# Second layer of three batch pairs as seven block products instead of eight, with weight blocks kept in DRAM

## The chip, the core and the metric

One core of a Trainium2 chip runs the whole program. The metric is the device time of one execution in microseconds (us), the median of several. The profile is of one execution; its times count from the start of its span.

## The reference

Eight batches of 448 tokens go through attention with 12 heads of 64, and then through a layer that is applied to 128 chosen tokens of each batch:

```python
attn = softmax(scale * rmsnorm(q, g_q) @ rmsnorm(k, g_k).T) @ v     # (8, 12, 448, 64), all fp32
x = attn.transpose(0, 2, 1, 3).reshape(8, 448, 768)
scores = x @ w_gate
for b in range(8):
    top_idx = the 128 tokens of batch b with the highest score
    xe = x[b, top_idx]                         # 128 x 768
    h = maximum(xe @ w1, 0)                    # w1 is 768 x 1024
    ye = h @ w2                                # w2 is 1024 x 768
    out[b, top_idx] = x[b, top_idx] + sigmoid(scores[b, top_idx]) * ye
```

The product h @ w2 is the "second layer" of the title.

## The kernel before

**Attention.** The function `fast` does the work. A unit is one 64-key block of one group of four heads; there are 24 groups (three for each batch) of seven units, 168 units in all. For a unit, `scores` (L294) writes two PSUM tiles with 64-row matmuls, ACT takes the exponential (L303), `values` (L318) multiplies by v, and DVE adds the probabilities up (L334) for the denominators. When a group has ended, `values_out` copies its two halves from PSUM (tile `xT`), `sum_keys` (L362) sums the denominators on PE, `invert_sums` (L386, L388) inverts them, `to_tokens` (L407) transposes each half c back to token order, and DVE scales it (L409). `gate` (L433) makes the score for the choice; after the last group of a batch `score_rows` (L462, L468), `count` (L478) and `annotate` rank the tokens, `select` (L505) scatters the chosen rows to DRAM on the POOL queue, `load_selected` (L523) reads them back, and `store_x` (L421) stores the batch.

**The layers.** Batches are taken in five groups: (0), (1, 2), (3, 4), (5, 6), (7). `mixture` is a generator; each `yield` ends one *piece*. A pair has two pieces of transposes (L553), eight of the first layer (L582, moving 256 columns, both tokens' batches at once) and eight of the second layer (L601): for each batch and each half of 384 output columns, eight fp32 matmuls over the 1024 inner rows, four to a piece, into one PSUM bank. DVE then adds gate times result to the tokens (L610), and POOL writes rows out (L620). An fp32 matmul of full width is two records in the profile.

**The order of work** is written out by hand. Round q takes units 4q to 4q+3: all their scores and values, then two halves. Each half may take one piece of the layers (`piece`) and one or two waiting tasks (`opening`): a group that ends in round q has `sum_keys` due at place 1 of round q, `to_tokens` of its first half at the start of round q+1 and `last_tokens` (its second half) at place 1 of round q+1. Work in `todo` is run at its slot; slots 4q to 4q+3 belong to round q, two to each half. DMAs of the SP queue are issued in that order too. `single` says in which rounds the second half takes no piece: always while the first group is under way (rounds below BEGIN = 21), and for a pair where the count of its pieces stands at 3 or 4. Rounds start in the profile at 106.1 us (q = 12), 157.0 (17), 197.0 (21), 276.1 (28), 314.0 (31), 393.1 (38). Pair (1, 2) runs in rounds 21 to 30, pair (3, 4) in 31 to 40; pair (5, 6) and batch 7 come after the last unit, from 440 us on.

**PSUM.** Eight banks of one tile each: four for `sc` (pool `ps_sc`, scores and some others), two for `av`, one `aux` (denominators, transposes of `to_tokens`) and one `moe` (the layers). After the last unit `bank()` takes the layers' banks from `sc`.

```python
def to_tokens(n, c):
    ...
    if c == 1 and not before_layers(now[0]) and not spare[0]:
        ps = ps_sc.tile(shape, F32, tag="sc", name="x_ps")
    else:
        ps = aux(shape, "x_ps")
```

Of the kernel before, what the change touches and what calls it, by code (L numbers as in the profile page):

```python
# [68 lines left out]
def fast(  # L69
# [100 lines left out]

    wg = const.tile([CP, DM], F32, name="wg")
    w1 = const.tile([128, NDC, F], F32, name="w1")
    w2 = const.tile([128, NFC, DM], F32, name="w2")
    earlier = const.tile([CP, NJ, NJ, CP], mybir.dt.bfloat16, name="earlier")
    token_i = const.tile([CP, NJ], I32, name="token_i")
    token_f = const.tile([CP, NJ], F32, name="token_f")
# [16 lines left out]
        nc.gpsimd.tensor_copy(out=token_f, in_=token_i)  # L193

    def load_w(part):
        for w, src in ((w1, moe_w1), (w2, moe_w2)):
            n = w.shape[1]
            if part < n:
                nc.sync.dma_start(
                    out=w[:, part], in_=src.rearrange("(c p) f -> p c f", p=128)[:, part]  # L200
                )
            part -= n
            if part < 0:
                return

    def squares(n, i):
        t = get("tok", n, i)
# [127 lines left out]

    def values_out(n):
        for c in (1, 0):
            t = norm_pool.tile([128, NJ, CP], F32, name="xT", bufs=4)  # L340
            nc.scalar.copy(out=t.rearrange("d j p -> d (j p)"), in_=avs[n][c][:, 0:S])
            xTs[n, c] = t
        avs.pop(n)
# [52 lines left out]
    def to_tokens(n, c):  # L396
        b = n // NG
        if b not in xs:
            xs[b] = x_pool.tile([CP, NJ, DX], F32, name="x")
        t = xTs.pop((n, c))  # L400
        shape = [128, NJ, 128]
        if c == 1 and not before_layers(now[0]) and not spare[0]:
            ps = ps_sc.tile(shape, F32, tag="sc", name="x_ps")
        else:
            ps = aux(shape, "x_ps")
        for j in range(NJ):
            nc.tensor.transpose(out=ps[:CP, j, :], in_=t[:, j, :], identity=ident)  # L407
        col = (n % NG * 2 + c) * 128
        nc.vector.tensor_tensor(  # L409
            out=xs[b][:, :, col : col + 128].rearrange("p j (h d) -> p j h d", d=D),  # L410
            in0=ps[:CP].rearrange("p j (h d) -> p j h d", d=D),
            in1=rdens[n][:, :, :, c, None].to_broadcast([CP, NJ, 2, D]),
            op=OP.mult,
        )
# [10 lines left out]
    def gate(n):  # L425

        b, g = divmod(n, NG)
        if g == 0:
            gates[b] = moe_pool.tile([CP, NJ, NG], F32, name="gate_parts", bufs=2)
        cols = slice(GH * D * g, GH * D * (g + 1))  # L430
        for j in range(NJ):
            prod = moe_pool.tile([CP, GH * D], F32, name="prod")
            nc.vector.scalar_tensor_tensor(  # L433
                out=prod,
                in0=xs[b][:, j, cols],
                scalar=1.0,
                in1=wg[:, cols],
                op0=OP.mult,
                op1=OP.mult,
                accum_out=gates[b][:, j, g : g + 1],  # L440
            )
# [88 lines left out]
    def mixture(g):  # L530

        n, bs = CAP, groups[g]
        G = len(bs)
        wide = 128 * G
        xe = [xes.pop(b) for b in bs]
        parts_out = 1 if bs[-1] < B - 1 else 3
        xeT = moe_pool.tile([128, NDC, 2, 128], F32, name="xeT")
        hT = moe_pool.tile([128, NFC, 2, 128], F32, name="hT")

        def bank():  # L540

            if PER * now[0] >= units:
                return ps_sc.tile([128, 512], F32, tag="sc", name="sc")
            return ps_moe.tile([128, 512], F32, tag="moe", name="moe_ps")

        half = NDC // 2
        rows = []
        for i, x in enumerate(xe):
            for a in range(2):
                ps = ps_sc.tile([128, 512], F32, tag="sc", name="xeT_ps") if a else bank()  # L550
                for d in range(half):
                    dc = half * a + d
                    nc.tensor.transpose(  # L553
                        out=ps[:, 128 * d : 128 * d + n],
                        in_=x[:n, 128 * dc : 128 * (dc + 1)],
                        identity=ident[:n, :n],
                    )
                nc.scalar.copy(  # L558
                    out=xeT[:, half * a : half * (a + 1), i, :n],
                    in_=ps[:, : half * 128].rearrange("p (i t) -> p i t", t=128)[:, :, :n],  # L560
                )
                if a == 1:
                    row = moe_pool.tile([128, parts_out], I32, name="row", bufs=4)
                    for part in range(parts_out):
                        nc.vector.tensor_scalar(
                            out=row[:n, part : part + 1],
                            in0=x[:n, DM + 1 : DM + 2],
                            scalar1=float(parts_out),
                            scalar2=float(part),
                            op0=OP.mult,  # L570
                            op1=OP.add,
                        )
                    rows.append(row)
                if a == 1 or G == 1:
                    yield

        chunks = 4 // G
        for f0 in range(0, NFC, chunks):
            ps = bank().rearrange("p (i g t) -> p i g t", g=G, t=128)
            for i in range(chunks):  # L580
                for dc in range(NDC):
                    nc.tensor.matmul(  # L582
                        out=ps[:, i, :, :n],
                        lhsT=w1[:, dc, 128 * (f0 + i) : 128 * (f0 + i + 1)],
                        rhs=xeT[:, dc, 0:G, :n],
                        start=(dc == 0),
                        stop=(dc == NDC - 1),
                    )
                if i == chunks // 2 - 1:
                    yield  # L590
            nc.scalar.activation(
                out=hT[:, f0 : f0 + chunks, 0:G, :n], in_=ps[:, :, :, :n], func=AF.Relu
            )
            yield
        width = DM // max(2, parts_out)
        for i, x in enumerate(xe):
            for c0 in range(0, DM, width):
                cols = slice(c0, c0 + width)
                ps = bank()
                for fc in range(NFC):  # L600
                    nc.tensor.matmul(  # L601
                        out=ps[:n, :width],
                        lhsT=hT[:, fc, i, :n],
                        rhs=w2[:, fc, cols],
                        start=(fc == 0),
                        stop=(fc == NFC - 1),
                    )
                    if fc == NFC // 2 - 1:
                        yield
                nc.vector.scalar_tensor_tensor(  # L610
                    out=x[:n, cols],
                    in0=ps[:n, :width],
                    scalar=x[:n, DM : DM + 1],
                    in1=x[:n, cols],
                    op0=OP.mult,
                    op1=OP.add,
                )
                if parts_out > 1 or c0 + width == DM:
                    part = slice(c0 if parts_out > 1 else 0, c0 + width)
                    nc.gpsimd.indirect_dma_start(  # L620
                        out=out.flatten_outer_dims().rearrange("r (k c) -> (r k) c", k=parts_out),
                        out_offset=bass.IndirectOffsetOnAxis(
                            ap=rows[i][:n, part.start * parts_out // DM :][:, :1], axis=0
                        ),
                        in_=x[:n, part],
                        in_offset=None,
                    )
                yield

    HALVES = 2  # L630
    PER = 2 * HALVES
# [4 lines left out]
    def at(slot, fn, *args):  # L636
        todo.setdefault(slot, []).append(lambda: fn(*args))
# [31 lines left out]
    for n in range(1, n_groups):  # L669
# [4 lines left out]
        if n > 1:  # L674
# [3 lines left out]
            first = max(s0 - (20 if n > 5 else 17), 0)  # L678
            prepare(n, first)
            at(max(s0 - 6, first + 11), scale_q, n)  # L680
    for part in range(NDC + NFC):
        at(16 + 3 * part, load_w, part)
    at(7, lambda: nc.sync.dma_start(out=wg, in_=_bcast_row(moe_w_gate, CP)))
    at(11, constants)

# [17 lines left out]
    def before_layers(q):  # L703
        return done == 0 and ready.get(0, q + 1) > q

    def soon():

        q, place = now
        return PER * q + 2 * place if PER * q < units else -9
# [69 lines left out]
    def single(q):  # L779

        if q in begin:
            return pieces[0] > 0
        return PER * q < units and pieces[1] > 10 and pieces[0] in (3, 4)

    def piece(q):

# [6 lines left out]
        if ready.get(done, q + 1) > q:  # L793
            return False
        moe = mixture(done)
        pieces[:] = 1, 2 + 8 * len(groups[done])
        done += 1
        next(moe)
        return True
# [567 lines left out]
```

## Time and profile before

| what | value |
|---|---|
| runs | 513.98, 515.16, 520.19 us; median 515.16 us |
| the profiled execution | 514.41 us, of which the span is 512.6 us |
| granted TensorE clock | 1.00 of full speed |
| busy time of PE, DVE, ACT, POOL | 499.2, 333.2, 274.2, 182.7 us |
| moved by DMA | 93.21 MB |

A timeline line reads: start, length, engine, line of the kernel, operation, output from inputs, partitions of the array, shape, and the number of instructions merged; in brackets the idle time before and what ended it. Lengths of matmul groups include the drain of the last one, so distances between starts are the better measure of what PE spends. PEld is the weight load of PE; DVE, ACT, POOL and SP are VectorE, ScalarE, GpSimd and SyncE.

### The profile page before, as it was taken

To read this page: it belongs to the slowest core of one execution; us is meant where nothing else is said; L and a number is where in the kernel's file an instruction comes from. 1 tells how busy PE (TensorE), PEld (TensorE's weight loads), DVE (VectorE), ACT (ScalarE), POOL (GpSimd) and SP (SyncE) were. 2 spreads that over 40 slices of the span, in tenths; PEclk is the share of its full clock that TensorE was granted. 3 is DMA by queue.
4 is the path that set the end of the run, shared out by engine and by line. 5 is a ranking of instruction groups with operands and counts; after the bars stand their busy time and mean duration, and the time that the engine had idled before them with its cause. 6 is when DMAs were issued, how large, how long until landed. Compare 5 with 4: busy or idle time off the path is not lost. (4 is left out here: it accounts for less than half of the span.)

```text
span 512.6 us, 11058 instructions
## 1 busy us (share of the span) xinstructions
PE 499.2 (97%) x4453; PEld 287.9 (56%) x4453; DVE 333.2 (65%) x638; ACT 274.2 (53%) x507; POOL 182.7 (36%) x104
## 2 busy tenths in 40 slices
PE   5999999989999999999999999999999999999996
PEld 4544455445555445556654454656564464786595
DVE  4566899699875998697746775798564675530101
ACT  4877886775766566575455544674643434310000
POOL 5694538445424283434422435137220131020102
PEclk9999999999999999999999999999999999999999
DMA  8977889999864578468258373587221042031001
GB/s 307 375 245 254 276 284 355 320 314 319 266 214 138 191 248 276 146 216 243 68 151 264 76 259 107 177 255 191 87 85 60 9 155 71 6 125 41 31 33 36
DMA packets 43405, 93.21 MB, mean 182 GB/s; under 512 B 11059, under 2 KB 23348, under 8 KB 43346
## 3 DMA queue, kind: packets, MB, share of 16 engines
q1 hardware_dynamic: 39938, 86.11, 52.5%
q0 software_dynamic: 3264, 6.31, 3.5%
q8 instruction: 37, 0.61, 0.5%
q14 instruction: 22, 0.18, 0.1%
q10 hardware_dynamic: 144, 0.00, 0.0%
HBM read 74.93 MB, written 25.35 MB: 196 GB/s over the span
## 5 line engine op out<-in xcount | busy, mean ns | idle before, releaser
L303 ACT ACTIVATE p<-sc,rinv 128x448 f32<-128x448 f32 x336 | 186.2, 642 | 98.4 <-PE sc L294 72.6
L222 POOL TENSOR_TENSOR rinv<-ss,neg_half 128x14 f32<-128x14 f32 (+1 forms) x49 | 131.9, 2699 | 185.8 <-DVE ss L221 154.9
L294 PE MATMUL sc<-qT,kT 64*64 64x448 f32 x1344 | 155.0, 545 | 1.7 <-DVE x L409 0.8
L318 PE MATMUL av<-p,v 64*64 64x448 f32 x1344 | 148.7, 537 | 0.0
L334 DVE TENSOR_TENSOR sum<-sum,p 128x896 f32<-128x896 f32 x107 | 116.5, 1089 | 8.8 <-ACT p L303 2.9
L318 PEld LDWEIGHTS av<-p,v 64*64 64x64 f32 x1344 | 59.9, 133 | 67.5 <-issue 58.4
L294 PEld LDWEIGHTS sc<-qT,kT 64*64 64x64 f32 x1344 | 54.3, 132 | 70.0 <-issue 43.5
L221 DVE TENSOR_REDUCE ss<-sq 128x14 f32<-128x910 f32 (+1 forms) x49 | 52.1, 1074 | 18.9 <-ACT sq L212 18.9
L582 PE MATMUL moe_ps<-xeT,w 128*128 128x256 f32 (+1 forms) x288 | 56.1, 347 | 0.0
L601 PE MATMUL moe_ps<-w,hT 128*128 128x384 f32 x160 | 55.7, 491 | 0.0
L505 POOL DMA_INDIRECT selected<-x,rank x32 | 34.4, 1076 | 55.4 <-DVE x L497 47.3
L409 DVE TENSOR_TENSOR x<-x_ps,rden 112x512 f32<-112x512 f32 x48 | 32.6, 689 | 30.5 <-PE x_ps L407 29.9
L582 PEld LDWEIGHTS moe_ps<-xeT,w 128*128 128x128 f32 x288 | 46.2, 191 | 7.3 <-issue 3.2
L212 ACT ACTIVATE sq<-tok 128x896 f32<-128x896 f32 (+1 forms) x49 | 46.0, 952 | 5.2 <-DMA tok<-in_tok_dram 2.9
L433 DVE SCALAR_TENSOR_TENSOR prod<-x,wg 112x256 f32<-112x256 f32 x96 | 40.6, 423 | 3.0
L620 POOL DMA_INDIRECT out_dram<-xe,row x10 | 11.6, 1156 | 81.9 <-DVE xe L610 63.1
L601 PEld LDWEIGHTS moe_ps<-w,hT 128*128 128x128 f32 x160 | 28.8, 190 | 18.7 <-issue 2.8
L610 DVE SCALAR_TENSOR_TENSOR xe<-sc,xe 128x384 f32<-128x384 f32 (+1 forms) x7 | 3.9, 560 | 48.1 <-PE sc L601 48.1
L582 PE MATMUL sc<-xeT,w 128*128 128x256 f32 (+1 forms) x192 | 32.2, 328 | 0.3 <-ACT xeT L558 0.3
L601 PE MATMUL sc<-w,hT 128*128 128x384 f32 (+1 forms) x112 | 31.3, 440 | 0.0
L582 PEld LDWEIGHTS sc<-xeT,w 128*128 128x128 f32 x192 | 28.8, 191 | 2.9 <-ACT xeT L558 0.5
L407 PE MATMUL x_ps<-ident,xT 128*112 128x128 f32 x192 | 28.8, 276 | 0.0
(67 smaller groups left out, 293.5 us busy)
## 6 DMA issues: line engine op xcount, KB each, us to landing
tok<-in_tok_dram SPq DMA_DIRECT2D x48, 448.0 KB, 6.7
qT<-in_qT_dram SPq DMA_DIRECT2D x24, 448.0 KB, 4.6
kT<-in_kT_dram SPq DMA_DIRECT2D x24, 448.0 KB, 7.5
v<-in_vp_dram SPq DMA_DIRECT2D x24, 448.0 KB, 8.6
out_dram<-x SPq DMA_DIRECT2D x8, 1344.0 KB, 7.3
bc<-rows SPq DMA_DIRECT2D x44, 224.0 KB, 5.8
xe<-selected SPq DMA_DIRECT2D x8, 385.0 KB, 3.7
w<-in_moe_w_dram SPq DMA_DIRECT2D x6, 512.0 KB, 7.0
```

The source lines that it names most:

```text
L212: nc.scalar.activation(out=sq[:, h, :, 0:D], in_=t[:, h], func=AF.Square, scale=scale)
L221: nc.vector.tensor_reduce(out=ss[:, h], in_=sq[:, h], axis=AX.X, op=OP.add)
L222: nc.gpsimd.tensor_tensor(out=rinv[:, h].rearrange(flat), in0=ss[:, h].rearrange(flat), in1=neg_half.to_broadcast([128, (h.stop - h.start) ...
L294: nc.tensor.matmul(out=scs[hh][D * c : D * (c + 1), 0:S], lhsT=get("kT", n)[r, c, D * i : D * (i + 1)], rhs=get("qT", n)[r, c, :], start=True,
L303: nc.scalar.activation(out=p[:, hh], in_=scs[hh][:, 0:S], func=AF.Exp, scale=rinvs[n, 1][:, hh, i : i + 1],)
L318: nc.tensor.matmul(out=avs[n][c][D * hh : D * (hh + 1), 0:S], lhsT=get("v", n)[r, hh, i, :], rhs=probs[u][r, hh], start=(i == 0), stop=(i ...
L334: nc.vector.tensor_tensor(out=sums[n], in0=probs.pop(u - 1) if begins else sums[n], in1=probs.pop(u), op=OP.add)
L409: nc.vector.tensor_tensor(out=xs[b][:, :, col : col + 128].rearrange("p j (h d) -> p j h d", d=D), in0=ps[:CP].rearrange("p j (h d) -> p j ...
L433: nc.vector.scalar_tensor_tensor(out=prod, in0=xs[b][:, j, cols], scalar=1.0, in1=wg[:, cols], op0=OP.mult, op1=OP.mult, accum_out=gates[b ...
L505: w = nc.gpsimd.indirect_dma_start(out=t[:, :], out_offset=bass.IndirectOffsetOnAxis(ap=rank[:, j : j + 1], axis=0), in_=x[:, j, :], in_of ...
L582: nc.tensor.matmul(out=ps[:, i, :, :n], lhsT=w1[:, dc, 128 * (f0 + i) : 128 * (f0 + i + 1)], rhs=xeT[:, dc, 0:G, :n], start=(dc == 0), sto ...
L601: nc.tensor.matmul(out=ps[:n, :width], lhsT=hT[:, fc, i, :n], rhs=w2[:, fc, cols], start=(fc == 0), stop=(fc == NFC - 1),)
```

## The change

With A the two batches' hidden rows (two halves of the inner dimension each) and B the four blocks of w2 (inner half by column half), the second layer of a pair is a 2 by 2 block product. The change does it with seven block products of four matmuls each (Strassen's scheme in Winograd's form). Four of the weight factors are mixed blocks, T1 = B12 - B11, T3 = B22 - B12, T2 = B22 - T1 and B21 - T2. DVE makes them once (`mix`), in halves, in rounds 20 to 23; they are stored in DRAM in halves (`store_mixed`) and read back into two buffers named `ring` when the pairs need them (`load_mixed`, by way of `reload`). Three w2 blocks stay in SBUF (B11, B21, B22); B12 is read into the ring at the start and again for batch 7. The factors on the side of the tokens, s1 to s4, are made by DVE for each pair, three of them in the room of `xeT`, s4 over a11.

The products in the rounds of attention are, one to a piece: a12 B21 (own bank), a11 B11 (bank `main`, `moe`), then s2 T2 added into `main`, s1 T1 (own bank), s4 B22 (own bank), s3 T3 added into `main`, a22 (B21 - T2) added into `main`. In the text they are P2, P1, P6, P5, P3, P7 and P4 in that order; after the last unit P1 comes before P2. The banks of P2, P5 and P3 come from `sc`. Each product is followed by one eviction into the tokens (`gated`), P5 by two. A pair has 17 pieces instead of 18.

Further parts: the round without a second piece moves from counts 3 and 4 to 13 and 14; in rounds that `single` names, the second half of `to_tokens` takes the `aux` bank; `xT` has three buffers instead of four; `prod` shares the buffer of `cmp`; batch 7's output goes in column parts of 384, 256 and 128 instead of three of 256; a pair's first batch is written after P3 and its second after P4.

```diff
-    w2 = const.tile([128, NFC, DM], F32, name="w2")
+    HF, HD = NFC // 2, DM // 2
+    w2 = {b: const.tile([128, HF, HD], F32, name=f"w2_{b[0]}{b[1]}") for b in ((0, 0), (1, 0), (1, 1))}
+    mixed = [dram_pool.tile([128, HF, HD], F32, name=f"mixed{i}", bufs=1) for i in range(4)]
...
+    def in_ring(what):
+        ring[what] = moe_pool.tile([128, HF, HD], F32, name="ring", bufs=2)
+        return ring[what]
...
+    def load_mixed(i, part):
+        dst = ring[i] if part else in_ring(i)
+        nc.sync.dma_start(out=dst[:, chunk(part)], in_=mixed[i][:, chunk(part)])
+
+    def store_mixed(i, part):
+        nc.sync.dma_start(out=mixed[i][:, chunk(part)], in_=ring[i][:, chunk(part)])
+
+    def mix(i, part):
...
+        nc.vector.tensor_tensor(out=ring[i][:, f], in0=a[:, f], in1=b[:, f], op=OP.subtract)
...
-            t = norm_pool.tile([128, NJ, CP], F32, name="xT", bufs=4)
+            t = norm_pool.tile([128, NJ, CP], F32, name="xT", bufs=3)
...
-        if c == 1 and not before_layers(now[0]) and not spare[0]:
+        if c == 1 and not (before_layers(now[0]) or spare[0] or now[1] == 1 and single(now[0])):
...
+        parts_out = ((0, HD), (DM - 2 * HD // 3, DM), (HD, DM - 2 * HD // 3)) if last else ((0, DM),)
...
+        spare_room = xeT.rearrange("p c g t -> p (c g t)").rearrange("p (s f t) -> s p f t", s=3, t=128)
+        s1, s2, s3, s4 = spare_room[0], spare_room[1], spare_room[2], a11
+        for o, p, q, op in ((s1, a21, a22, OP.add), (s2, s1, a11, OP.subtract), (s3, a11, a21, OP.subtract)):
+            nc.vector.tensor_tensor(out=o[:, :, :n], in0=p[:, :, :n], in1=q[:, :, :n], op=op)
+
+        def product(ps, h, w, first=True):
+            for f in range(HF):
+                nc.tensor.matmul(
+                    out=ps[:n, :HD],
+                    lhsT=h[:, f, :n],
+                    rhs=w[:, f],
+                    start=first and f == 0,
+                    stop=(f == HF - 1),
+                    skip_group_check=True,
+                )
+
+        def side():
+            return ps_sc.tile([128, 512], F32, tag="sc", name="side_ps")
+
+        def reload(i):
+            s = soon()
+            for part in range(2):
+                at(s + 4 + 2 * part if s >= 0 else s, load_mixed, i, part)
+
+        main = ps_moe.tile([128, 512], F32, tag="moe", name="moe_ps")
+        for first in (0, 1) if PER * now[0] < units else (1, 0):
...
+            yield
+        product(main, s2, ring[2], first=False)
+        gated(0, high, main)
+        reload(3)
+        yield
+        ps = side()
+        product(ps, s1, ring[1])
+        gated(1, high, ps)
+        gated(0, high, ps)
+        reload(0)
+        yield
+        ps = side()
+        product(ps, s4, w2[1, 1])
+        gated(0, high, ps)
+        write(0, 0)
+        yield
+        product(main, s3, ring[3], first=False)
+        gated(1, high, main)
+        if g < len(groups) - 2:
+            reload(2)
+        else:
+            for part in range(2):
+                at(soon(), load_block, (0, 1), part)
+        yield
+        product(main, a22, ring[0], first=False)
+        gated(1, low, main)
+        write(1, 0)
+        if g < len(groups) - 2:
+            reload(1)
+        yield
...
+    mixing = PER * (BEGIN - 1) + 2
+    for k, i in enumerate((3, 1, 2, 0)):
+        for part in range(2):
+            at(mixing + 3 * k + part, mix, i, part)
+            at(mixing + 3 * k + part + 2, store_mixed, i, part)
+    for part in range(2):
+        at(mixing + 16 + 2 * part, load_mixed, 1, part)
...
-        return PER * q < units and pieces[1] > 10 and pieces[0] in (3, 4)
+        return PER * q < units and pieces[1] > 10 and pieces[0] in (13, 14)
...
-        pieces[:] = 1, 2 + 8 * len(groups[done])
+        pieces[:] = 1, 10 if len(groups[done]) == 1 else 17
```

## The prediction

> **What bounds the kernel.** I read the page first: its span, its busy times and the row of each engine in 40 slices.
>
> ```profile
> span 512.6 us, 11058 instructions
> PE 499.2 (97%) x4453; PEld 287.9 (56%) x4453; DVE 333.2 (65%) x638; ACT 274.2 (53%) x507; POOL 182.7 (36%) x104
> PE   5999999989999999999999999999999999999996
> DVE  4566899699875998697746775798564675530101
> PEclk9999999999999999999999999999999999999999
> ```
>
> PE is full in nearly every slice at full clock. Busy time counts drains, so I checked with distances between starts in the timeline: in a round of attention 64 records (16 scores, 16 values, twice) take 6.2 us, and rounds from 13 on are these plus their pieces, with some tenths over. So PE sets the pace, and work taken from PE shortens the time unless its place is filled by a wait. DVE is at 90% in places, so waits on DVE are what I look for.
>
> **Gross gain.** The timeline of the stretch after the last unit shows one pair's second layer with nothing between:
>
> ```profile
> 464.71 20.80 PE L601 MATMUL sc<-w,hT 128*128 128x384 f32 x64
> 485.36 0.49 PE L553 MATMUL sc<-ident,xe 128*128 128x128 f32 x3
> ```
>
> 64 records take 485.36 - 464.71 = 20.65 us, 0.3227 us each. Eight block products of four matmuls (8 records) become seven: 8 x 0.3227 = 2.58 us per pair, 7.74 us for three pairs. That is the ceiling of the main effect. The schedule does not undo it: round 30 has one piece where it had two, and the next pair still starts in round 31, since its `ready` is set by `ranks_of` in round 28 either way.
>
> **What takes some of it back.** The seven pieces stand closer together than the eight did, in one bank and in rounds without a second piece.
>
> 1. *Main bank, pair (5, 6).* P4 adds into `main` directly after P7, and must wait until DVE has read P7's result. During attention six us of scores stand between; after the last unit nothing does. The row for this eviction:
>
> ```profile
> 485.56 0.62 DVE L610 SCALAR_TENSOR_TENSOR xe<-sc,xe 128x384 f32<-128x384 f32 x1 [4.54 <-PE sc L601]
> ```
>
> It starts 0.20 us after the next matmul would start and lasts 0.62; with 0.1 to release PE, 0.92 us are lost.
>
> 2. *Aux bank, round 17.* `to_tokens` c = 1 now takes `aux` there, and `sum_keys` wants `aux` next (first PE, then DVE):
>
> ```profile
> 166.38 0.60 PE L407 MATMUL x_ps<-ident,xT 128*112 128x128 f32 x4
> 166.91 0.59 PE L362 MATMUL den_ps<-sum,pick_pair 128*32 128x112 f32 x16
> ```
>
> ```profile
> 167.01 0.69 DVE L409 TENSOR_TENSOR x<-x_ps,rden 112x512 f32<-112x512 f32 x1 [2.02 <-PE x_ps L407]
> ```
>
> The bank is free at 167.70, so L362 starts at about 167.75 instead of 166.91: 0.84 us.
>
> 3. *The same in round 38,* which is now one without a second piece (count 14):
>
> ```profile
> 402.29 0.60 PE L407 MATMUL x_ps<-ident,xT 128*112 128x128 f32 x4
> 402.73 2.75 PE L601 MATMUL moe_ps<-w,hT 128*128 128x384 f32 x8
> 405.40 0.59 PE L362 MATMUL den_ps<-sum,pick_pair 128*32 128x112 f32 x16
> ```
>
> Today 2.67 us of matmuls cover L409. In the new order P5 ends at 402.29, DVE first makes P5's two evictions (402.45 to 403.6), then L409 to 404.3; L362 follows at 404.35 instead of 402.73: 1.62 us. Of the six rounds in which `last_tokens` and `sum_keys` meet (3, 10, 17, 24, 31, 38), only 17 and 38 are `single`.
>
> 4. *Bank of P5, round 28.* The counts stand in DVE's queue ahead of P5's evictions:
>
> ```profile
> 282.26 0.59 PE L462 MATMUL row_ps<-ident,gate 112*112 112x112 f32 x4
> 285.38 0.59 PE L362 MATMUL den_ps<-sum,pick_pair 128*32 128x112 f32 x16
> 285.90 2.85 PE L601 MATMUL moe_ps<-w,hT 128*128 128x384 f32 x8
> ```
>
> ```profile
> 283.45 0.69 DVE L478 SCALAR_TENSOR_TENSOR cmp<-score_rows,gate,earlier 112x448 f32<-112x448 f32 x1 [2.82 <-ACT score_rows L468]
> 287.19 1.10 DVE L221 TENSOR_REDUCE ss<-sq 128x14 f32<-128x910 f32 x1
> ```
>
> The piece at 285.90 falls away, so round 29 starts there. A unit's 8 score records take 0.75 us; the second unit, from 286.65, wants the bank that P5 holds. Counts and the scaling of q end at 287.2, the two evictions (0.55 apart) at 288.4: up to 1.8 us if that very bank is taken, about 0.9 if one freed by an exponential is taken, nothing if counts come earlier. I take 1.0.
>
> **DVE's new work.** No row shows these additions; the nearest are L334 with 896 columns (1.09 us) and L478 with 448 (0.69), 0.9 ns per column. Mixing is 8 x 768 columns at 0.97, 7.8 us in rounds 20 to 23; s1 to s4 are 4 x 512 at 0.75, 3.0 us per pair; evictions go from 4 to 8, 2.5 us per pair. Sum 24 us, on PE's path only where something waits. DVE is busy 9.1 of 10.6 us in round 20 and 8.1 of 8.7 in round 21, so it runs some 2 us late there. What is late next: the last sum before L362 of round 21 moves from 201.8 to 203.7, and L362 is at 204.17, so it holds. In rounds 22 and 23 the second piece, added by the move of counts 3 and 4, gives DVE 2.7 us each. Without this cover the lateness (about 2 us) would pass to PE. I take 0.3, range 0 to 2.
>
> A rule speaks against this. The Trainium skill, "SBUF — State Buffer", section "Who interferes with whom", says that a DVE instruction with two SBUF inputs contends with a GpSimd one that reads SBUF, and that the later one blocks. The rows:
>
> ```profile
> L334 DVE TENSOR_TENSOR sum<-sum,p x107: 1026/1092/1145, 22.9 to 439.4; 128x896 f32<-128x896 f32 x107
> POOL rinv L222 <- DVE ss L221: 154.9, 28, 14.1
> ```
>
> L334 has two SBUF inputs and runs 107 times beside L222 (2.7 us each, POOL 36% busy), yet spreads over 0.12 us only. By the rule, 7 of the 20 new instructions would wait half an L222, 9 us of DVE, and some 2 to 4 us on PE; by the row, nothing. I take the row. POOL has 155 us of slack if it is the one that waits.
>
> **SP's queue and the weight blocks.** 8 stores, 22 loads of mixed halves and 2 more of B12 are new, 0.39 MB each, 0.35 to 0.6 us of SP per issue. Stores wait for `mix` two slots after it, in a time in which SP issues nothing for over 7 us (202.2 to 209.76). `mix` of T2 waits until T3 is stored, `mix` of the last block until T1 is: 3 slots, about 7 us, each; roughly a landing, in the 0.3. T3 and the P4 block are asked for one round after P6 and P5, and used 2 to 2.5 rounds after: over 8 us. The long wait in the queue (`store_x` of batch 6 behind a row write, 27.2 us) comes at slot 158 after the load of the same slot, so the loads pass it. Behind it stand only loads wanted after 440 us. I take nothing; if loads were late, P7 and P4 would stand, and scores behind them.
>
> After the last unit T3's load starts only when P6 has ended, and P7 comes two products (5.16 us) later. The rows for such sizes (median to landing):
>
> ```profile
> w<-in_moe_w_dram SPq DMA_DIRECT2D x8, 384.0 KB, 9.2
> xe<-selected SPq DMA_DIRECT2D x8, 385.0 KB, 3.7
> ```
>
> The Trainium skill, "DMA: Bandwidth & Descriptors", section "Anatomy of one DMA", gives about 2.0 us fixed plus bytes over 436 GB/s (for GpSimd's path): an estimate of 3.8 us for both halves, no wait; its section "Bandwidth" asks for 1 MiB per transfer. By the w row, taken while DMA was at 70 to 90%, the second half would come 9.6 us after P6, wanted at 6.45: 3.1 us lost. Late in the run DMA is idle, so I take the xe row: no wait.
>
> **At nothing.** Weights as three tiles (loads in the same slots, same bytes); `prod` in the room of `cmp` (both written by DVE in turn); `xT` with three buffers: ACT's second copy waits for a transpose that PE runs within 1 us, with no exponential behind it. Scores no longer wait for L409 in rounds 12 and 14, but c = 1 waits for c = 0 instead: gain 0.2. Batch 7's parts: 16 records each of 0.3227, 0.216 and 0.113 (rows of 384, 256 and 128 columns) give 10.42 against 48 x 0.216 = 10.37; the last eviction is 0.13 shorter and the last write half as large: gain 0.2.
>
> **Sum.** 7.74 + 0.2 + 0.2 - 0.92 - 0.84 - 1.62 - 1.0 - 0.3 = 3.46 us. The profiled execution, 514.41 us (span 512.6 and 1.8 around it), would become 510.95. The median of the runs is 0.75 above it: 515.16 - 3.46 = 511.7.
>
> **Rivals.** *Little is given back* (25%): the waits of rounds 17, 28 and 38 vanish because DVE is ahead or another bank is taken; only the main bank's 0.92 and 0.3 remain: 7.74 + 0.4 - 1.2 = 6.9, 508.2. For it: DVE works only 3.9 of the 12.9 us of round 37, so it enters round 38 with nothing behind. Against: the order of `aux` is fixed.
> *Blocks come late* (12%), slower than before: the ring's loads stand behind other SP work and land after P7 or P4 should start. Pairs (1, 2) and (3, 4) have two such places each, pair (5, 6) two more. It decides from 3.5 us in sum, 0.6 at each of six. At the w row's excess, 3.1 us twice in pair (5, 6), and the DVE share above, it is 515.16 - 3.46 + 6.2 = 517.9. Against: the idle DMA rows.
> *The removed matmuls were cover for DVE everywhere* (8%): DVE's 24 us delays sums and banks in every round of the pairs, all 7.7 us turn into waits: 515.
>
> **Numbers.** 55% for the forecast, 511.7. The range takes in the 508.2 case with its own 0.7 and reaches over 515 into the late cases: 507.5 to 515.5. The forecast alone would be 509.5 to 513.5. A gain over 2% (10.3 us, about what can be told from no change) needs more than the ceiling: 3%. A loss over 2% needs several late blocks: 3%.
>
> **What would show it.** 56 records of second-layer matmuls per pair; waits of PE for L409 in rounds 17 and 38, for an eviction before P4 near the end and for P5's bank in round 29; none for a ring load. The prediction is wrong if PE waits for DMA of the ring, if rounds 20 to 23 are over their sum by more than 1 us, or if those four waits are absent.

## The result, and the profile after

| kernel | median of the runs | lowest to highest | ratio to the kernel before (95% interval) |
|---|---|---|---|
| before | 515.4 us (22 runs) | 513.85 to 520.61 | |
| changed | 513.1 us (22 runs) | 511.77 to 517.7 | 0.9946 (0.992 to 0.9971) |

Some 2.3 us less by the medians, 1.5 to 4.1 by the interval, where 3.46 were forecast. The profiled execution took 513.42 us. The page after, answering to the rows shown first of the kernel before:

```profile
span 511.7 us, 11121 instructions
PE 491.6 (96%) x4429; PEld 279.4 (55%) x4429; DVE 354.0 (69%) x670; ACT 274.8 (54%) x507; POOL 187.0 (37%) x104
DVE  4566898699866898996687886777567686623201
```

PE lost 24 records (three pairs of eight) and 7.6 us of busy time, DVE gained 20.8 us; the sum of additions forecast 24. PE's gain reached the end only in part. In the text below, line numbers are those of the changed kernel: scores L328, sum L368, denominators L396, `to_tokens` L441 and L443, counts L512, evictions L596, row writes L587, mixing L240, products L683.

The four waits that were forecast are there. First, the last pair (timelines of PE and of DVE): P7 starts at 475.76, P4 should at 478.34 and starts at 479.22, after the eviction.

```profile
475.76 2.74 PE L683 MATMUL moe_ps<-ring,xeT 128*128 128x384 f32 x8
479.22 2.85 PE L683 MATMUL moe_ps<-ring,hT 128*128 128x384 f32 x8 [0.71 <-DVE xe L596]
```

```profile
478.55 0.62 DVE L596 SCALAR_TENSOR_TENSOR xe<-moe_ps,xe 128x384 f32<-128x384 f32 x1 [1.96 <-PE moe_ps L683]
```

Second, round 17: L396 stands behind DVE's reading of the aux bank.

```profile
167.54 0.69 DVE L443 TENSOR_TENSOR x<-x_ps,rden 112x512 f32<-112x512 f32 x1 [2.07 <-PE x_ps L441]
```

```profile
168.29 0.59 PE L396 MATMUL den_ps<-sum,pick_pair 128*32 128x112 f32 x16 [0.79 <-DVE x L443]
```

Third, round 38, where DVE makes P5's two evictions first, in the order that was forecast:

```profile
404.54 1.14 DVE L596 SCALAR_TENSOR_TENSOR xe<-side_ps,xe 128x384 f32<-128x384 f32 x2 [1.89 <-PE side_ps L683]
405.60 0.68 DVE L443 TENSOR_TENSOR x<-x_ps,rden 112x512 f32<-112x512 f32 x1
```

```profile
406.33 0.59 PE L396 MATMUL den_ps<-sum,pick_pair 128*32 128x112 f32 x16 [1.40 <-DVE x L443]
```

Fourth, rounds 28 and 29: P5 ends at about 289.4, and its evictions wait behind four counts until 291.16, in a round that starts at 289.87. The scores of its second unit come late, so that its first 13 score records are spread over 2.44 us:

```profile
291.16 1.14 DVE L596 SCALAR_TENSOR_TENSOR xe<-side_ps,xe 128x384 f32<-128x384 f32 x2
```

```profile
289.87 2.44 PE L328 MATMUL sc<-qT,kT 64*64 64x448 f32 x13
```

No PE wait names a ring load. What was not forecast is at the end. The last matmul ends at 507.82 in the profile before and at 504.39 in that after, yet the spans end at 512.6 and 511.7. The row writes on POOL, before and after:

```profile
502.13 0.96 POOL L620 DMA_INDIRECT out_dram<-xe,row  x1 [14.72 <-DVE xe L610]
505.62 0.96 POOL L620 DMA_INDIRECT out_dram<-xe,row  x1 [2.52 <-DVE xe L610]
508.78 0.96 POOL L620 DMA_INDIRECT out_dram<-xe,row  x1 [2.21 <-DVE xe L610]
```

```profile
500.51 0.95 POOL L587 DMA_INDIRECT out_dram<-xe,row  x1 [16.55 <-DVE xe L596]
504.15 0.96 POOL L587 DMA_INDIRECT out_dram<-xe,row  x1 [2.69 <-issue]
507.96 0.96 POOL L587 DMA_INDIRECT out_dram<-xe,row  x1 [2.85 <-issue]
```

Before, evictions came 3.45 us apart, and the profile names DVE for each write. But in its chain of the work that ended last, the third write follows the second write's DMA and not the eviction:

```profile
505.62 0.96 DMA out_dram<-xe,row
506.58 1.98 issue
508.78 0.96 POOL out_dram L620
```

In the trace POOL waits, ahead of the second and the third write, for the semaphore of the write ahead, which tells of its landing. The two start 1.09 and 0.76 us after that landing before, 1.09 and 0.77 us after it in the changed kernel. Before, each write landed 2.40 us after its start, so the starts are 3.49 and 3.16 us apart: the pace of the landings was the pace of the evictions, and cost nearly nothing. After, the first two landed 2.55 and 3.04 us after their starts, so the starts are 3.64 and 3.81 us apart, whatever the evictions do, which end at 499.81, 503.12 and 504.78. The last eviction is done at 504.78 and its write starts at 507.96.

The stretches, by the distances between starts of rounds in the two profiles:

| stretch | forecast | measured |
|---|---|---|
| eight products to seven, three pairs | -7.74 | -7.74 (by count, with seven 2.58 apart) |
| rounds 11 to 14 | -0.2 | -0.11 |
| round 17, aux bank | +0.84 | +0.86 |
| round 29, P5's bank | +1.0 | +1.19 |
| round 38, aux bank | +1.62 | +1.57 |
| main bank of the last pair | +0.92 | +0.88 |
| mixing, pieces moved, all other rounds | +0.3 | -0.7 |
| from the last matmul to the end | -0.2 | +2.53 |
| sum | -3.46 | -1.5 |

The profile after starts round 0 0.64 us later than that before (11.48 against 10.84), so its span is only 0.9 us shorter. The -0.7 is what is left of the whole; it is spread over several rounds and was not traced. Of the -0.11 little can be said, since these rounds differ by more from execution to execution.

### The profile page after: what moved, and what is told of

It is laid out like the page before. It is cut to its first block, busy times and chain, and to the rows that moved or that the text cites. A ratio compares the mean times of both kernels' runs of the same rounds, so it can differ in the third digit from the quotient of the medians.

```text
span 511.7 us, 11121 instructions
## 1 busy us (share of the span) xinstructions
PE 491.6 (96%) x4429; PEld 279.4 (55%) x4429; DVE 354.0 (69%) x670; ACT 274.8 (54%) x507; POOL 187.0 (37%) x104
## 5 line engine op out<-in xcount | busy, mean ns | idle before, releaser
L256 POOL TENSOR_TENSOR rinv<-ss,neg_half 128x14 f32<-128x14 f32 (+1 forms) x49 | 135.7, 2775 | 184.4 <-DVE ss L255 164.9
L328 PE MATMUL sc<-qT,kT 64*64 64x448 f32 x1344 | 152.7, 545 | 1.0 <-DVE qT L307 0.8
L352 PE MATMUL av<-p,v 64*64 64x448 f32 x1344 | 147.0, 537 | 0.0
L368 DVE TENSOR_TENSOR sum<-sum,p 128x896 f32<-128x896 f32 x107 | 116.5, 1089 | 8.1 <-ACT p L337 1.9
L352 PEld LDWEIGHTS av<-p,v 64*64 64x64 f32 x1344 | 57.6, 133 | 69.6 <-issue 62.3
L328 PEld LDWEIGHTS sc<-qT,kT 64*64 64x64 f32 x1344 | 52.5, 132 | 69.3 <-issue 43.8
L539 POOL DMA_INDIRECT selected<-x,rank x32 | 35.8, 1118 | 47.7 <-DVE x L531 39.7
L443 DVE TENSOR_TENSOR x<-x_ps,rden 112x512 f32<-112x512 f32 x48 | 32.5, 687 | 20.8 <-PE x_ps L441 18.3
L587 POOL DMA_INDIRECT out_dram<-xe,row x10 | 10.5, 1052 | 85.7 <-DVE xe L596 67.9
L441 PE MATMUL x_ps<-ident,xT 128*112 128x128 f32 x192 | 28.8, 276 | 2.0 <-DVE x L443 2.0
L287 DVE SCALAR_TENSOR_TENSOR qT<-qT,gg,bc 128x896 f32<-128x896 f32 x22 | 25.3, 1149 | 4.4 <-DMA bc<-rows 4.4
L512 DVE SCALAR_TENSOR_TENSOR cmp<-score_rows,gate,earlier 112x448 f32<-112x448 f32 x32 | 21.9, 684 | 9.1 <-ACT score_rows L502 8.1
L441 PEld LDWEIGHTS x_ps<-ident,xT 128*112 128x112 f32 x192 | 21.8, 134 | 10.3 <-issue 4.5
L368 DVE TENSOR_TENSOR sum<-p 128x896 f32<-128x896 f32 x24 | 25.9, 1078 | 1.8 <-ACT p L337 1.8
```

The costliest lines, as they stand in the source:

```text
L256: nc.gpsimd.tensor_tensor(out=rinv[:, h].rearrange(flat), in0=ss[:, h].rearrange(flat), in1=neg_half.to_broadcast([128, (h.stop - h.start) ...
L328: nc.tensor.matmul(out=scs[hh][D * c : D * (c + 1), 0:S], lhsT=get("kT", n)[r, c, D * i : D * (i + 1)], rhs=get("qT", n)[r, c, :], start=True,
L352: nc.tensor.matmul(out=avs[n][c][D * hh : D * (hh + 1), 0:S], lhsT=get("v", n)[r, hh, i, :], rhs=probs[u][r, hh], start=(i == 0), stop=(i ...
L368: nc.vector.tensor_tensor(out=sums[n], in0=probs.pop(u - 1) if begins else sums[n], in1=probs.pop(u), op=OP.add)
L443: nc.vector.tensor_tensor(out=xs[b][:, :, col : col + 128].rearrange("p j (h d) -> p j h d", d=D), in0=ps[:CP].rearrange("p j (h d) -> p j ...
L539: w = nc.gpsimd.indirect_dma_start(out=t[:, :], out_offset=bass.IndirectOffsetOnAxis(ap=rank[:, j : j + 1], axis=0), in_=x[:, j, :], in_of ...
```

## The experiments

Each is the changed kernel with one edit or several; ratios are to the kernel before. One thing has to be known to read them: rounds 10 to 13 differ from execution to execution, in most versions without an edit there. DVE's scaling of q (L287) waits for a row broadcast to land, in two places, and round 14 starts at 126.4 to 133.3 us in the fourteen profiles. The two ends, as waits of DVE between 84 and 134 us, first of the version with P4 in a bank of its own, then of that with the sums made twice:

```profile
DVE qT L287 <- DMA bc<-rows: 0.8, 1, 0.8
```

```profile
DVE qT L288 <- DMA bc<-rows: 8.6, 2, 5.2
```

So single profiles are compared round by round, and ratios only where they differ by more than this leaves open.

### The end of the program

```diff
-        parts_out = ((0, HD), (DM - 2 * HD // 3, DM), (HD, DM - 2 * HD // 3)) if last else ((0, DM),)
+        parts_out = ((0, HD), (HD, DM)) if last else ((0, DM),)
```

> One part of the change altered: batch 7's output in two column parts of 384 instead of 384, 256 and 128. In the changed kernel the last matmul starts at 503.3 and ends at 504.4, its eviction ends at 504.8, but POOL starts the third row write only at 507.96, 3.8 us after the second (504.15), and the span ends 3.7 us after that. Theory (each row write waits until the one before it has landed, since all go to one tensor): with two parts 5.2 us apart the second write starts 0.45 us after its eviction, near 505.5, and the span ends near 509.3, 2.4 us (2.0 to 2.8) earlier than in the changed kernel: ratio to the kernel before about 0.990. Rival (the end is longer for another reason, such as slow issue or a late execution): under 0.5 us of difference, ratio 0.994 to 0.996.

Measured: 510.46 us, ratio 0.9912 (0.9888 to 0.9936). The last matmul ends at 505.66 and the span at 510.7: 5.04 us, against 7.31. POOL's two last lines:

```profile
501.86 0.96 POOL L587 DMA_INDIRECT out_dram<-xe,row  x1 [16.55 <-DVE xe L596]
506.60 0.96 POOL L587 DMA_INDIRECT out_dram<-xe,row  x1 [3.78 <-DVE xe L596]
```

The last write again follows its eviction (505.70 to 506.32): with 5.2 us between evictions the landing ahead, 2.8 us after its start, is over. The 2.3 us come back in the profile (1.8 by the ratios, whose intervals overlap a little). Next, one write of whole rows, with nothing ahead of it:

```diff
-        parts_out = ((0, HD), (DM - 2 * HD // 3, DM), (HD, DM - 2 * HD // 3)) if last else ((0, DM),)
+        parts_out = ((0, DM),)
...
-                if last or h:
-                    write(0, k if last else 0)
+                if h:
+                    write(0, 0)
```

> Batch 7's rows are computed in two halves of 384 columns and written once, whole, after the second eviction, so that at the end no write has another ahead of it on its way. Theory (each write of rows to the result waits until the one ahead has landed): the end after the last matmul goes from 7.31 us to about 5.2 (eviction 0.7, write 1.0, landing 3.1 to 3.5), some 2.1 us less than the changed kernel, about 0.991 of the kernel before. Rival (the write of the whole row lands later, because it carries three to six times the bytes): 6 us or more after the last matmul, about 0.993 or above.

Measured: 512.61 us, ratio 0.9945 (0.992 to 0.997). The write starts 0.7 us after the eviction (507.67), but lands 3.5 us after that start, where the last write of 384 columns took 2.7 and that of 128 took 2.3; the span ends 1.4 us after the last landing in each of the three. The end is 6.29 us. The rival holds here: nothing to wait for, but a whole row lands later. Freeing the three narrow writes from each other was not tried.

### The bank of to_tokens

First the condition of the kernel before, everywhere:

```diff
-        if c == 1 and not (before_layers(now[0]) or spare[0] or now[1] == 1 and single(now[0])):
+        if c == 1 and not before_layers(now[0]) and not spare[0]:
```

> One part of the change undone: the second half of to_tokens takes a score bank again in all rounds. Theory (aux is the wait in rounds 17 and 38): round 17 falls from 11.26 to about 10.4 us and round 38 from 11.87 to 10.3 to 10.7; rounds 11 to 14 are the same in sum within 0.3; net 2.0 us (1.2 to 2.5) faster than the changed kernel, ratio to before about 0.991. Rival (the bank is needed: scores now wait for it, since P5 and P3 hold score banks): rounds 38 and 39 gain nothing or lose, net within 0.7 us, ratio 0.993 to 0.996.

Measured: 512.7 us, ratio 0.9934 (0.991 to 0.9958). Against the changed kernel that is 0.6 us, well inside the intervals, so only the rounds can tell. Round 17 returns to 10.40 us and round 38 to 10.40; rounds 21, 28 and 39 grow by 0.18, 0.19 and 0.18. Round 14 takes 11.05 us (10.61 in the kernel before), against 9.57 in all twelve profiles with the aux bank there; how much of this rounds 12 and 13 give back can't be told, since they vary. Next, the score bank in rounds 17 and 38 alone:

```diff
-        if c == 1 and not (before_layers(now[0]) or spare[0] or now[1] == 1 and single(now[0])):
+        if c == 1 and not (before_layers(now[0]) or spare[0] or now[1] == 1 and now[0] < 16 and single(now[0])):
```

> Only the rounds 17 and 38 take a score bank again for the second half of to_tokens (c = 1); rounds 12 and 14 keep the changed kernel's bank. Theory (the aux bank is the price of these two rounds): round 17 returns from 11.26 to 10.40 us and round 38 from 11.87 to about 10.4, some 0.4 us of it given back in rounds 28 and 39; 1.9 us less than the changed kernel, about 0.991 of the kernel before. Rival (the score bank's reader is as late as the aux bank's, so the wait only moves to the scores): rounds 18 and 39 grow by what 17 and 38 lose, no gain, about 0.995.

Measured: 514.37 us, ratio 0.996 (0.9938 to 0.9982). By rounds: 17 loses 0.86 us and 38 loses 1.47, rounds 28 and 39 gain 0.37 together, round 18 nothing: 1.96 us, the theory. The ratio doesn't show it. This kernel, the two of the next section and the first one with all edits ran on a chip of their own (the kernel before stood at 516.59 us there), and their profiles have 0.7 to 1.2 us more in round 20, 0.3 in round 21 and 0.7 to 0.8 in round 34, where no edit is. (In round 21, 0.18 of it may be the score bank's here, as in the version before.) The changed kernel was not run beside them, and what lengthens those rounds was not pursued.

### The bank of P4, and P5's evictions

```diff
-        product(main, a22, ring[0], first=False)
-        gated(1, low, main)
+        if PER * now[0] < units:
+            product(main, a22, ring[0], first=False)
+            gated(1, low, main)
+        else:
+            gated(1, low, main)
+            ps = side()
+            product(ps, a22, ring[0])
+            gated(1, low, ps)
```

> In the last pair alone the seventh product goes to a bank of its own, and the result of the product before it is added to the rows twice (one eviction more on DVE). Theory (the eviction of P7 holds P4 for 0.9 us): P4 starts 2.58 us after P7 and all that follows comes 0.9 us earlier, about 0.993 of the kernel before. Rival (the further eviction holds the banks of batch 7's first layer): the 0.9 us come back within the next ten us, about 0.995.

Measured: 514.18 us, ratio 0.9975 (0.9954 to 0.9996). In PE's timeline P7 starts at 476.87 and P4 2.57 us later, without a wait:

```profile
479.44 2.74 PE L683 MATMUL side_ps<-ring,hT 128*128 128x384 f32 x8
```

From the pair's first product to the next transposes it is 18.06 us instead of 19.04, and from round 41 to the end of the last matmul 74.80 instead of 75.77; nothing of the 0.97 us is given back. The ratio again carries the longer rounds of this chip (1.4 us in rounds 20 and 21 and 0.8 in round 34 of this profile, 0.4%).

```diff
-        at(s + 1, count, b, (2, 3))
+        at(s + (2 if pieces[1] > 10 and pieces[0] >= 12 else 1), count, b, (2, 3))
```

> In rounds 28 and 39 the second two counts are asked for behind the piece of the second layer instead of ahead of it, so P5's two evictions stand behind two counts and the scaling of q alone. Theory (scores of round 29 wait for P5's bank): the evictions start at about 289.5 instead of 291.2 and round 29 goes from 13.55 to about 12.4; round 39 likewise gains up to 0.5; 1.2 to 1.7 us less than the changed kernel, about 0.992 of the kernel before. Rival (the exponentials behind the squares on ACT set round 29): round 29 keeps its length, about 0.995; if ranks come late, more.

Measured: 515.95 us, ratio 0.9984 (0.9959 to 1.0009). Round 29 goes from 13.55 to 12.86 us; round 39 keeps 12.86 and round 40 grows by 0.19. Timelines of DVE and of PE, in a round that starts at 290.91:

```profile
290.87 1.14 DVE L596 SCALAR_TENSOR_TENSOR xe<-side_ps,xe 128x384 f32<-128x384 f32 x2
```

```profile
290.91 1.75 PE L328 MATMUL sc<-qT,kT 64*64 64x448 f32 x13
```

So the lateness of P5's evictions is the cause of 0.69 of the 1.19 us. Which bank the scores waited for is another matter. In the trace the late scores of the changed kernel (291.71) are released by an exponential that ended at 291.66, as in the forecast's case of "one freed by an exponential"; here they are released at 292.02 by P5's second eviction, 0.35 us later after the start of the round than the second unit comes in the kernel before. The rest of the remaining 0.5 us stays open. For round 39 the expectation was wrong, and the ratio shows no gain.

### DVE's additions

Twice the work (T1, made in place, stays single):

```diff
-        nc.vector.tensor_tensor(out=ring[i][:, f], in0=a[:, f], in1=b[:, f], op=OP.subtract)
+        for _ in range(1 if i == 1 else 2):
+            nc.vector.tensor_tensor(out=ring[i][:, f], in0=a[:, f], in1=b[:, f], op=OP.subtract)
...
-        for o, p, q, op in ((s1, a21, a22, OP.add), (s2, s1, a11, OP.subtract), (s3, a11, a21, OP.subtract)):
+        for o, p, q, op in 2 * ((s1, a21, a22, OP.add), (s2, s1, a11, OP.subtract), (s3, a11, a21, OP.subtract)):
```

> DVE's sums doubled: each mix except the one in place and s1 to s3 are computed twice over, 5.7 us more DVE in rounds 20 to 23 and 2.1 us per pair, 12 us in all; results unchanged. Theory (DVE's new work lies beside PE, only banks in a fixed order wait): 0.5 us slower than the changed kernel (0 to 1.5), in rounds 21 to 24. Rival (DVE's lateness is what takes back the gain, all through the pairs): at least 4 us slower, since 12 us are added to the 24 that the change brought.

Measured: 516.87 us, ratio 1.0018 (0.9998 to 1.0037), 3.7 us more than the changed kernel by the ratios. By rounds, round 21 takes 1.37 us more and round 23 0.89, which is 2.3 us where the blocks are mixed. Rounds 24 to 40 take 0.14 more together, and the stretch from round 41 to the last matmul 0.38: the doubled token sums s1 to s3, some 6 us of DVE over the three pairs, cost half a microsecond. The other 0.9 us lie in what varies before round 14, as far as one profile tells. My expectation of 0.5 (up to 1.5) fell, but the rival's "all through the pairs" did too. Then none of the mixing:

```diff
-        nc.vector.tensor_tensor(out=ring[i][:, f], in0=a[:, f], in1=b[:, f], op=OP.subtract)
+        if i == 2:
+            load_mixed(2, part)
...
-        nc.sync.dma_start(out=dst[:, chunk(part)], in_=mixed[i][:, chunk(part)])
+        src = moe_w2.rearrange("(k f p) (h c) -> k h p f c", p=128, f=HF, c=HD)[0, 1]
+        nc.sync.dma_start(out=dst[:, chunk(part)], in_=src[:, chunk(part)])
...
-            at(mixing + 3 * k + part + 2, store_mixed, i, part)
```

> Leaves out the mixing of the weight blocks (8 DVE subtractions) and its 8 stores; the ring's loads stay, in the same places, and bring a block of the second weight matrix as it is instead of a mixed one, so the products are those of other blocks. Theory (the mixing lies almost wholly beside PE): rounds 20 to 23 lose 0.3 to 0.6 us, and nothing else moves; about 0.994 of the kernel before. Rival (DVE has no room in rounds 20 to 23, as the doubled sums showed): 2 us or more, 0.991 or less.

Measured: 513.14 us, ratio 0.9957 (0.9936 to 0.9979), no faster than with the mixing. Rounds 21 and 23 in three kernels: stretch, length, then busy time of PE, PEld, DVE, ACT and POOL with counts, TensorE clock, DMA share and GB/s. The changed kernel:

```profile
198.39:206.88 8.49, 8.37 (x93) 4.12 (x92) 8.35 (x17) 7.17 (x15) 2.49 (x2) 1.00 0.70 194
219.37:232.54 13.17, 13.17 (x110) 8.16 (x109) 12.45 (x30) 8.36 (x16) 3.94 (x2) 1.00 0.99 329
```

Without mixing:

```profile
201.64:210.13 8.49, 8.37 (x93) 4.12 (x92) 8.03 (x18) 7.17 (x15) 2.55 (x2) 1.00 0.88 288
222.62:235.80 13.18, 13.18 (x111) 8.17 (x110) 9.90 (x24) 8.36 (x17) 2.84 (x1) 1.00 0.66 207
```

With the doubled sums:

```profile
202.55:212.41 9.86, 8.37 (x93) 4.12 (x92) 9.65 (x18) 7.27 (x15) 2.49 (x2) 1.00 0.63 189
224.90:238.96 14.06, 13.84 (x110) 8.25 (x109) 13.64 (x27) 8.47 (x16) 0.86 (x1) 1.00 0.80 278
```

The mixing costs PE nothing: rounds 20 to 23 take 44.78 us with it and 44.79 without, and round 23 is 13.2 us long with DVE busy for 9.9 or for 12.4. With DVE at 95% of that round and 98% of round 21 its room is just used up, and of the same work again, 5.7 us, 2.3 go to PE's path.

### When ring loads do come late

```diff
-        return PER * q < units and pieces[1] > 10 and pieces[0] in (13, 14)
+        return PER * q < units and pieces[1] > 10 and pieces[0] in (3, 4)
```

> One part of the change undone: the rounds without a second piece are again those at counts 3 and 4 (22, 23, 32, 33), so P1 to P4 of a pair lie two to a round. Theory (P5's bank in round 29 and aux in round 38 wait because no piece covers DVE): these two waits, 1.19 and 1.57 us, go; against it DVE's mixing in rounds 20 to 23 has 5.2 us less time and may cost PE 0.5 to 2 us, and T3 and the last block, asked for one round after P6 and P5, come only just before P7 and P4: up to 1 us. Net 0.5 us faster (from 2.5 faster to 1.5 slower than the changed kernel), ratio about 0.994. Rival (the blocks come late by way of DRAM): PE waits for ring loads in rounds 29 and 39 with 2 us or more each, slower than the kernel before.

Measured: 522.38 us, ratio 1.0143 (1.0109 to 1.0177). Of the two waits that this schedule was to remove, that of round 38 went, and round 29 kept 13.35 us of its 13.55; the 0.5 to 2 us that the mixing was to cost did not come either. From round 12 to round 40 the shift against the changed kernel is only 0.2 us; the loss is in round 40 (16.75 us instead of 8.90). PE's wait, then SP's queue:

```profile
PE moe_ps L683 <- DMA ring<-mixed: 6.3, 1, 6.3
```

```profile
402.70 0.82 SPq L221 DMA_DIRECT2D ring<-mixed  x2
422.16 0.62 SPq L455 DMA_DIRECT2D out_dram<-x  x1
422.84 14.22 SPq L221 DMA_DIRECT2D ring<-mixed  x5
```

The store of batch 6 (L455) waits 18.6 us for a row write to land, and the block for P4 stands behind it in the queue. Then the same schedule with that store asked for four slots later:

```diff
...
-        at(s + 4 if s >= 0 else s, store_x, b)
+        at((s + 8 if b == B - 2 else s + 4) if s >= 0 else s, store_x, b, xs[b])
```

> The pieces are let go near the start of each pair (pieces 3 and 4, as in the earlier run with them) and the store of batch 6's result is asked for four slots later. Theory (that run lost 6.3 us because the last block's load stood in SP's queue behind that store, which waits for a write of rows): round 40 returns from 16.75 to about 9 us, and the kernel stands at about 0.999 to 1.001 of the kernel before, since its pairs' last products still stand in rounds with two pieces. Rival (the load itself is late, by its own release): no more than 1 us comes back, 1.012.

Measured: 519.93 us, ratio 1.0086 (1.0057 to 1.0115). Round 40 is back at 8.90 us, so the store was the cause, but from the start of round 41 to the last matmul it takes 6.35 us more. The store waits again, and now the load of batch 6's chosen rows is what stands behind it, issued at 437.68:

```profile
PE sc L610 <- DMA xe<-selected: 4.6, 1, 4.6
```

I had priced only the load that I moved the store away from, not the next one in the queue.

### All together

Score bank in rounds 17 and 38, P4 in a bank of its own, counts split, batch 7 in two halves:

> The score bank in rounds 17 and 38, P4 of the last pair in a bank of its own, the second two counts behind the piece, and batch 7 written in two halves. Theory (four separate prices): the gains add, 1.9 + 0.9 + 1.2 + 2.4 = 6.4 us less than the changed kernel, about 0.982 of the kernel before (506 us). Rival (some are the same DVE lateness in another place): 0.986 or more.

Measured: 509.34 us, ratio 0.9858 (0.9836 to 0.9879), faster than both kernels, but short of the 6.4 us expected against the changed kernel. By rounds: 0.86 (17), 0.70 (29) and 1.47 (38) less, 0.56 more in rounds 28, 39 and 40, 0.97 less up to the last matmul and 1.4 less at the end (5.91 us), 4.8 in all. The end is 0.9 us short of the version with two halves alone, since the first of its two last writes landed 4.4 us after its start instead of 2.8 and the second had to wait for it (their starts 5.48 us apart instead of 4.74). With one write of whole rows in place of the two halves:

> The four edits together, with batch 7's rows written once instead of in two halves. Theory (a write with none ahead of it ends soonest): the end after the last matmul is about 5.2 us against 5.9 in the profile of the version with two halves, 0.985 of the kernel before or a little less. Rival (the first half's landing is hidden behind the second half's matmuls, and half a row lands sooner than a whole one): the same or up to 0.5 us more than with two halves, 0.986 or 0.987.

Measured: 510.89 us, ratio 0.9889 (0.9851 to 0.9927); the end is 6.25 us. Nothing speaks for the whole row; two halves are better or the same.

## Why the prediction was right, and where not

**Gross gain.** Right: 2.58 us a pair, seen as seven products 2.58 us apart; the schedule did not undo it.

**The four waits.** Right in place, order and size, within 0.05 us in rounds 17 and 38 and in the last pair; undoing them gave back 0.86, 1.47 and 0.97 us. In round 29, P5's evictions were named rightly, and 0.69 of the 1.19 us are shown to be theirs.

**DVE's new work.** Of "I take 0.3, range 0 to 2" for the mixing the low end is right: it costs nothing. The cover that the second pieces were to give in rounds 22 and 23 ("Without this cover the lateness (about 2 us) would pass to PE") was not needed. The version that lets the pieces go early mixes in the same rounds without second pieces in them; its rounds 22 and 23 are as long as in the kernel before (9.89 and 10.29 us), and PE waits for nothing there:

```profile
207.75:217.64 9.89, 9.89 (x87) 5.74 (x86) 9.54 (x14) 5.79 (x11) 4.58 (x2) 1.00 0.86 313
217.64:227.92 10.28, 10.28 (x98) 5.84 (x97) 10.00 (x21) 7.07 (x14) 3.71 (x1) 1.00 0.88 297
```

DVE is at 97% there, and the doubled sums show how little room that leaves.

The sum mean of L368 is 1089 ns as before, beside POOL, so on DVE's side the row of the trace was the right choice over the rule of the Trainium skill ("SBUF — State Buffer", "Who interferes with whom"), from which the prediction had made 2 to 4 us on PE's path. The rule is there all the same, but on POOL's side alone, where the prediction counted the slack but looked at no durations. Most of POOL's `rinv` (L256) take 2.58 us. The two that start while DVE mixes take 4.26 and 4.03:

```profile
209.04 4.26 POOL L256 TENSOR_TENSOR rinv<-ss,neg_half 128x14 f32<-128x14 f32 x1 [7.99 <-DVE ss L255]
216.45 4.03 POOL L256 TENSOR_TENSOR rinv<-ss,neg_half 128x14 f32<-128x14 f32 x1 [3.15 <-DVE ss L255]
```

The same two without mixing:

```profile
210.20 3.38 POOL L242 TENSOR_TENSOR rinv<-ss,neg_half 128x14 f32<-128x14 f32 x1 [5.83 <-DVE ss L241]
218.94 2.58 POOL L242 TENSOR_TENSOR rinv<-ss,neg_half 128x14 f32<-128x14 f32 x1 [5.36 <-DVE ss L241]
```

So it was POOL that waited, 2.3 us in these two, and no round of PE grew by it; the slack that the prediction named covers it.

**Ring loads.** Right: no wait, for the reason given (the store of batch 6 comes after the load of the same slot). The page's row for them:

```profile
ring<-mixed SPq DMA_DIRECT2D x22, 384.0 KB, 5.3
```

In the last pair T3's load is issued at 470.80 and P7 starts at 475.76 on time, so the landing there was under 5 us. The trace tells the landing of both halves for the P4 block: 4.1 us after the first was issued (473.38 to 477.52), near the prediction's estimate of 3.8. The rival "blocks come late" is real one schedule further on, at 6.3 us.

**The end: the term that was mis-sized.** "The last eviction is 0.13 shorter and the last write half as large: gain 0.2." It cost 2.5 us. I had priced the last part as if it were alone. The kernel before held the warning: its chain of the end went through the landing of the write ahead, with writes 3.49 and 3.16 us apart where evictions were 3.45 apart. Narrowing the last parts put the evictions 3.3 and 1.7 us apart, and the landings no longer hid behind them. Two halves take away 2.3 of the 2.5 us in the profile.

**The sum** missed by 2.7 us at the end and, the other way, by 1.0 us in the small rounds; by the medians the change gained 2.3 us instead of 3.5. That the result lies so near the forecast is in part luck, since the two errors have opposite signs and the 1.0 us was not explained. And the stated range, 507.5 to 515.5, takes in the kernel before as well: it could not have told the gain from none.

## What to carry to other kernels

When the last output is cut into parts, compare the distance between their evictions with the landing of one write and the restart after it (here 2.3 to 3.0 and 0.8 to 1.1 us): where the writes wait for each other, parts that come faster than that queue up, and cutting finer makes the end later. The engine that a profile names for such a write need not be the only one that held it. Before a load is trusted to be early, follow its queue for an instruction that waits on something late, and after moving that one, price the next load behind it. When a removed stretch of PE work is a bank's or a DVE reader's cover, the wait that appears can be worked out from the order of instructions on DVE, here to a tenth of a microsecond for three waits of four. And when two engines may hold each other up, look at the rows of both.

## What was not expected of the hardware

Row writes from GpSimd to one tensor, each waiting for the one ahead, started 3.6 to 3.8 us apart when their data was ready sooner, although each keeps POOL for 0.96 us only. From start to landing, 128 columns took 2.3 us, 384 columns 2.6 to 2.8 (4.4 once) and 768 columns 3.5. An addition on DVE with both inputs in SBUF held up a POOL instruction that started during it, by up to 0.8 us for a sum of L368 (3.36 to 3.39 us instead of 2.58) and by 0.9 and 1.5 us more with mixing; DVE's sums took 1.09 us beside POOL as alone. The landing of the broadcast rows in rounds 10 to 13 makes DVE wait between 0.8 and 8.6 us from one execution to another, more than the whole change is worth.
